# The last contraction chunk of a feature tile and of a key or query tile, side by side in the two halves of TensorE's rows

## The chip, the core and the metric

The kernel runs on one core of one Trainium2 chip. The metric is the device time of one execution in microseconds (us); the time before is the median of three runs. The engines named below are TensorE (PE; its weight loads are shown apart as PEld), VectorE (DVE), ScalarE (ACT), GpSimd (POOL) and SyncE (SP), which here only issues DMA transfers.

## What is computed

Two branches work on the same 2048 rows of `x`, with 448 features: linear attention with 16 heads of width 28, and a dense layer with a squared ReLU (1792 hidden features). A gate per row mixes them. Cut to what matters:

```python
g = sigmoid((x * gate_w).sum(-1, keepdims=True))
q, k, v = split(x @ wqkv)                    # 448 -> 3 * 448, 16 heads
phi = lambda t: where(t > 0, t + 1, exp(t)) + 1e-6
kv  = einsum("bhsd,bhse->bhde", phi(k), v);  z = phi(k).sum(over s)
a = (phi(q) @ kv / (phi(q) @ z + 1e-6)) @ wo
h = maximum(x @ w1 + b1, 0) ** 2             # 448 -> 1792
b = h @ w2 + b2                              # 1792 -> 448
out = g * a + (1 - g) * b
```

## The kernel before

**Precision by splitting.** Matrices are multiplied as `float32r`. To keep float32 precision each operand is kept as a high part and a low part (the rest), so a product of two 128-row chunks takes three matmuls: high by high, high by low, low by high.

**The contraction of 448.** Products with `x` (feature tiles of the dense layer, keys, queries) contract over 448 = 3 x 128 + 64. Chunks 0 to 2 have three matmuls each. The last chunk has 64 rows only, and the host puts them there twice, in partitions 0 to 63 and again in 64 to 127 (`twice`, L751). On chip the first copy of the weights is kept as high parts and the second as low parts (`split_w`, L126), while of `x` one tile holds high over low and the other low over high (`split_last`, L76). So two matmuls over all 128 rows (`xh[:, 3]` and `xl[:, 3]` against `w[:, 3]`) make all four products of the last chunk. A tile of outputs takes 3 x 3 + 2 = 11 matmuls.

**Three kinds of such tiles.** `up(b, f)` (L244) makes a feature tile: 128 hidden features by a block of 512 rows of `x`, moving operand 512 wide, into a PSUM bank `h_ps`; `hidden` (L234) then lets ACT take ReLU and square, and DVE split the result. `keys(t)` (L283) makes a tile of 128 rows by 448 keys, moving operand 448 wide, in `k_ps`. `queries(b, c)` (L433) makes 128 query columns by 512 rows in `q_ps`; its tile `c = 3` is narrower in precision (7 matmuls) and has a swap of partitions through DMAs. `keys` and `queries` return their later steps, which stand in the list `todo` until `run_todo` (L514) runs them: `phi` (L278, an exponential on ACT and two operations on DVE), for keys also splits (`rest`, L303), for queries the sum for the denominator.

**Other matmuls.** `down(b, f)` (L252) adds the products of feature tile `f` with `w2` to four accumulators `o_ps` (12 matmuls, 448 wide). `gram` (L320) sums the products of `x` and keys, `attention` (L497) applies the attention matrix to the scaled queries, `kv_product` (L385) and `m_product` (L411) build that matrix, `key_sums` makes `z_ps`, `denominators` makes `d_ps`. At L179 TensorE is kept busy with 15 matmuls until data arrives.

**Order.** The order on PE, ACT and DVE is written by hand (`manual_schedule`, L172): each engine runs its instructions in the order of the program's text. DMAs wait in SP's queue in program order too. The start (L521 to L595) treats block 0; the first half (L597) treats blocks 1 to 3, each with seven feature tiles `f`: `run_todo`, `up(b, f)`, `down` of the feature tile before, then a key tile for `f < 4` or `gram` after that. The second half (L656) takes the blocks in the order 3, 0, 1, 2 with the other seven feature tiles; there `up` and `down` alternate with `queries`, `scaled` (L485), `attention` and `finish` (L268). PSUM has eight banks: four `o_ps`, two for `up` (`mm`), and two (`ms0`, `ms1`) that keys, gram, queries and attention take in turn through `bank` (L48).

**What the steps below touch:** `split_w` and `split_wq` (last chunk), `terms_x`, `terms_w`, `products`, `up`, `keys`, `queries`, `run_todo`, `split_den` (L467), and the calls in the three stages. Working buffers in SBUF are slots of one pool (`slot`, L54): a load waits until the last reader of its slot is done.

Of the kernel before, what the change touches and what calls it, by code (L numbers as in the profile page):

```python
# [8 lines left out]
R = mybir.dt.float32r  # L9
# [6 lines left out]
P = 128  # L16
TB = 512
# [13 lines left out]
def gated_mix_kernel(ctx: ExitStack, tc: tile.TileContext, xt, xn, wk, wq, wv, wo, w1a, w1b, w2, b1, b2, gw, hmask,  # L31
# [28 lines left out]

    def split_hi(eng, hi, src):
        if eng is act:
            act.activation(hi, src, AF.Copy)  # L65
        elif eng is pool:
            pool.tensor_scalar(hi, src, 1.0, 0.0, op0=ALU.mult, op1=ALU.add)
        else:
            eng.tensor_copy(hi, src)  # L69
# [8 lines left out]
        dve.scalar_tensor_tensor(straight, src, sign[:, 1:2], f32(crossed), op0=ALU.mult, op1=ALU.subtract)  # L78
        split_lo(dve, crossed, src, straight)

    def products(out_ps, terms):
        n = len(terms)
        for i, (a, b) in enumerate(terms):
            pe.matmul(out_ps, a, b, start=(i == 0), stop=(i == n - 1))  # L84


    def terms_x(xh, xl, cols, w, wcols, c):
        if c == 3:
            return [(xh[:, 3, cols], w[:, 3, wcols]), (xl[:, 3, cols], w[:, 3, wcols])]
        return [(xh[:, c, cols], w[:, c, wcols]), (xh[:, c, cols], w[:, 4 + c, wcols]),  # L90
                (xl[:, c, cols], w[:, c, wcols])]

    def terms_w(xh, xl, w, wcols):
        t = []
        for c in range(3):
            t += [(w[:, c, wcols], xh[:, c]), (w[:, c, wcols], xl[:, c]), (w[:, 4 + c, wcols], xh[:, c])]
        return t + [(w[:, 3, wcols], xh[:, 3]), (w[:, 3, wcols], xl[:, 3])]

# [19 lines left out]
        else:  # L118
            split_last(xh[:, 3], xl[:, 3], r, side)

    def split_w(w, c, src, hi_eng, lo_eng):
        split_hi(hi_eng, w[:, c], src)
        if c < 3:
            split_lo(lo_eng, w[:, 4 + c], src, w[:, c])
        else:
            split_lo(lo_eng, w[64:, 3], src[64:], w[64:, 3])  # L126


    w1_s, w1_raw = {}, {}
# [6 lines left out]

    def new_w1(h, g):
        n, a, z = ((TB, 0, 16), (3 * P, 48, 0))[g]
        w = keep.tile([P, a + 7 * n + z], R, name=f"w1_{h}{g}", tag=f"w1{g}", bufs=1)
        w1_s[h, g] = w[:, a:a + 7 * n].rearrange("p (c n) -> p c n", c=7)  # L140
        return w1_s[h, g]

    def split_w1(h, g, c):
# [97 lines left out]
        split_lo(dve, lo, r, h)  # L241
        hs[f] = (h, lo)

    def up(b, f):  # L244
        ps = mm_p.tile([P, 512], F, name=f"h_ps{b}_{f}", tag="mm")
        for c in range(4):
            up_chunk(ps, b, f, c)
        hidden(ps, b, f)

    o_ps = {}  # L250
# [29 lines left out]
        dve.tensor_scalar(r, ps, 0.0, 1e-6, op0=ALU.max, op1=ALU.add)  # L280
        dve.scalar_tensor_tensor(p, e, 1.0, r, op0=ALU.min, op1=ALU.add)  # L281

    def keys(t):  # L283
        b, i = divmod(t, 4)
        if t < 2:
            ps = (acc_p, mm_p)[t].tile([P, 512], F, name=f"k_ps{t}", tag=("acc", "mm")[t])
        else:
            ps = bank(f"k_ps{t}")
        products(ps[:, :D], [term for c in range(4)
                             for term in terms_x(*xs[b], slice(i * P, (i + 1) * P), wk_s, slice(0, D), c)])  # L290
        e = slot([P, D], F, f"e{t}")
        r = slot([P, D], F, f"r{t}")
        p = r
        ph = tmp_p.tile([P, D], R, name=f"ph{t}", tag="ph", bufs=4)
        pl = tmp_p.tile([P, D], R, name=f"pl{t}", tag="pl", bufs=4)

        if t == 0:
            pool.memset(tmp_p.tile([P, 48], F, name="off"), 0.0)

        def first():  # L300
            phi(ps[:, :D], e, r, p)

        def rest():  # L303
            nh = tmp.tile([P, 512], R, name=f"nh{t}", tag="nh", bufs=4)
            nl = tmp.tile([P, 384], R, name=f"nl{t}", tag="nl", bufs=4)
            raw = xn_raw.pop(t)
            split_hi(act, nh[:, :D], raw)
            split_lo(pool, nl, raw[:, :384], nh[:, :384])
            split_lo(pool, nh[:, D:], raw[:, 384:], nh[:, 384:D])
            dve.scalar_tensor_tensor(e, raw, 1.0, gw_s, op0=ALU.mult, op1=ALU.mult, accum_out=logit[:, t:t + 1])  # L310
            split_hi(act, ph, p)
            split_lo(dve, pl, p, ph)
            if t == 0:
                pool.tensor_copy(ksum, p)
            else:
                pool.tensor_tensor(ksum, ksum, p, op=ALU.add)  # L316
            pend[t] = (ph, pl, nh, nl)
        return [first, rest]
# [15 lines left out]
                dve.tensor_tensor(gsum[c], ps[:, :D], gsum[c], op=ALU.add)  # L334
        return [after]

    wq_s = keep.tile([P, 8 + 7 * TB], R, name="wq_s")[:, 8:]
    wq_s = wq_s.rearrange("p (c n) -> p c n", c=7)
    wq_raw = {}

    def load_wq(c):
# [5 lines left out]
    def split_wq(c):  # L347
        raw = wq_raw.pop(c)
        split_hi(act, wq_s[:, c], raw)
        if c < 3:  # L350
            split_lo(dve, wq_s[:, 4 + c, :384], raw[:, :384], wq_s[:, c, :384])
        else:
            split_lo(dve, wq_s[64:, 3, :384], raw[64:, :384], wq_s[64:, 3, :384])
# [76 lines left out]

    pq, qs, den = {}, {}, {}

    def queries(b, c):  # L433
        ps = bank(f"q_ps{b}_{c}")
        xh, xl = xs[b]
        cols = slice(c * P, (c + 1) * P)
        if c < 3:
            products(ps, terms_w(xh, xl, wq_s, cols))
        else:
            products(ps, [(wq_s[:, i, cols], x[:, i]) for i in range(4) for x in ((xh, xl) if i < 3 else (xh,))])  # L440
        e = slot([P, TB], F, f"qe{b}_{c}")
        r = slot([P, TB], F, f"qr{b}_{c}")
        v = slot([P, TB], F, f"qv{b}") if c == 3 else None
        pq[b, c] = e

        def after():
            phi(ps if c < 3 else v, e, r, e)
            if (b, "s") not in den:
                den[b, "s"] = slot([P, TB], F, f"ds{b}")
                dve.tensor_scalar(den[b, "s"], e, zc[:, c:c + 1], None, op0=ALU.mult)  # L450
            else:
                dve.scalar_tensor_tensor(den[b, "s"], e, zc[:, c:c + 1], den[b, "s"], op0=ALU.mult, op1=ALU.add)  # L452
# [12 lines left out]
        return [swap if c == 3 else after]  # L465
# [45 lines left out]

    todo = []

    def run_todo():  # L514
        now, todo[:] = sorted(todo, key=lambda step: step.__name__ == "join"), []
        for step in now:
            todo.extend(step() or ())

# [22 lines left out]
                up_chunk(first[f], 0, f, c)  # L541
    split_w2(0)
    split_w2(1)
    wk_s = keep.tile([P, 7, D], R, name="wk_s", tag="wkm", bufs=1)
    for c in range(4):
        split_w(wk_s, c, wk_raw[c], act, dve)
    load(gw_s, gw.partition_broadcast(P))
    load(b2_s, b2.partition_broadcast(P))
    hidden(first[0], 0, 0)
# [18 lines left out]
    load_w2(4)  # L568
    load_x(1, 0)
    run_todo()  # L570
    up(0, 4)
    down(0, 2)
    todo += keys(2)
    load_xn(3)
    load_w2(5)
    load_x(1, 1)
    split_w2(4)
    run_todo()
    up(0, 5)
    down(0, 3)  # L580
    todo += keys(3)
    load_w2(6)
    load_x(1, 2)
    split_x(1, 0)
# [12 lines left out]
    for b in range(1, NB):  # L597
        for f in range(NH):
            run_todo()
            up(b, f)  # L600
            if f == 0:
                down(b - 1, NH - 1)
                half_done(b - 1)
                if b == 1:
                    for c in range(1, 4):
# [6 lines left out]
            if f < 4:  # L612
                if f < 3:
                    load_xn(4 * b + f + 1)
                todo += keys(4 * b + f)
            elif f < 6:
                todo += gram(b, f - 4)
            else:
# [37 lines left out]
    for n, b in enumerate(order):  # L656
        then = order[n + 1] if n + 1 < NB else None
        for f in range(NF - NH, NF):
            fl = f - NH
            run_todo()  # L660
            if fl == (0 if n else 4) and n != 1:
                split_den(b)
            up(b, f)
            if fl == 0 and n == 1:
                split_den(b)
            if then is not None and n and fl < 2:
                load_x(then, 2 * fl)
                load_x(then, 2 * fl + 1)
# [27 lines left out]
            else:  # L696
                down(order[n - 1], NF - 1)
                for i in range(4):
                    if n == 1:
                        attention(order[0], i)  # L700
                    finish(order[n - 1], i)
            if n == 0:
                if fl < 4:
                    todo += queries(b, (3, 0, 1, 2)[fl])
                if fl == 0:
                    for c in range(4):
                        load_w1(1, 1, c)
# [3 lines left out]
                    m_s = keep.tile([P, 7, D], R, name="m_s", tag="wkm", bufs=1)  # L711
                    split_kv(raw)
                    for j in range(2):
                        load_wo(j)
# [4 lines left out]
                if fl >= 4:  # L719
                    for c in ((3,), (0,), (1, 2))[fl - 4]:  # L720
                        todo += queries(then, c)
                if fl == 4:
                    todo += denominators(b)
                elif 2 <= fl < 6:
# [1 line left out]
            else:  # L726
# [7 lines left out]
                if then is not None and 3 <= fl:  # L734
                    todo += queries(then, (3, 0, 1, 2)[fl - 3])
    last = order[-1]
    down(last, NF - 2, range(3))
    for i in range(4):
# [55 lines left out]
```

## Time and profile before

| what | value |
|---|---|
| median of three runs | 437.86 us (437.72 to 438.6) |
| the profiled execution, its own time | 437.56 us |
| span of that execution, first to last instruction | 435.8 us |
| TensorE clock granted | 1.000 |
| DVE busy / ACT busy / POOL busy | 286.5 / 174.0 / 70.7 us |
| matmuls in the program | 2051 |
| DMA traffic | 29.00 MB in 18459 packets, mean 67 GB/s |

The page of the profile gives each engine's busy time as a share of the span. Matmuls are pipelined and the ends in the records are modelled: successive ones overlap, so a matmul's own duration is longer than the time between two starts, and it is the latter that adds up to the span. The chain of waits follows the work that ended last backwards, and gives for each piece its start, its length and its count; a piece of eleven matmuls divided by eleven is that time between starts.

### The profile page before, as it was taken

The page shows a single profiled execution, that of the slowest core. Times are in us where ns is not written, and L with a number is a line of the kernel's source. Part 1 is how long each engine was busy: PE and PEld are TensorE (multiplying, and loading weights), DVE is VectorE, ACT ScalarE, POOL GpSimd, SP SyncE. Part 2 cuts the span into 40 slices and gives each one's busy share as a digit, 9 for nine tenths or more (in the row PEclk, how much of TensorE's full clock was granted, in tenths as well). Part 3 has the DMA queues.
Part 4 walks back from the last instruction along what each step waited for, and adds up shares of the span by engine and source line. Part 5 has one row for each costly group of instructions (what it writes and reads, how often), then busy time and mean ns, then how long its engine had stood idle before and what let it go on. Part 6 is the DMA issues. An engine that isn't in the chain of part 4 may idle for free.

```text
span 435.8 us, 5547 instructions
## 1 busy us (share of the span) xinstructions
PE 430.4 (99%) x2051; PEld 380.7 (87%) x2051; DVE 286.5 (66%) x460; ACT 174.0 (40%) x301; POOL 70.7 (16%) x92
## 2 busy tenths in 40 slices
PE   9999999999999999999999999999999999999996
PEld 6888999898989898889888888888888888888985
DVE  5999537743779337883459778877653967457624
ACT  5855323421436123452245543444423434233421
POOL 0045013500234002540011342000100001000000
PEclk9999999999999999999999999999999999999999
DMA  7742202020131211132233321130101301002002
GB/s 271 249 133 70 89 0 70 25 68 28 42 120 31 68 45 64 49 84 84 80 123 112 71 62 37 55 128 0 26 0 48 135 0 26 0 0 86 0 2 84
DMA packets 18459, 29.00 MB, mean 67 GB/s; under 512 B 2896, under 2 KB 12928, under 8 KB 18432
## 3 DMA queue, kind: packets, MB, share of 16 engines
q1 hardware_dynamic: 16704, 26.51, 19.0%
q0 software_dynamic: 1728, 2.13, 2.3%
q8 instruction: 16, 0.26, 0.3%
q14 instruction: 11, 0.09, 0.1%
HBM read 22.31 MB, written 3.67 MB: 60 GB/s over the span
## 4 chain that ended last, share of the span: by engine, by line
PE 93%; DVE 4%; ACT 1%; DMA 1%; issue 0%; DVEq 0%; ACTq 0%
PE h_ps L232 31%; PE o_ps L261 30%; PE g_ps L84 8%; PE k_ps L84 8%; PE q_ps L84 7%; PE a_ps L84 7%; PE warm_ps L180 1%; PE kv_ps L389 1%; DVE qe L281 1%; DMA w2r<-in_w 1%; PE m_ps L84 1%; DVE ds L452 1%; DVE ql L72 0%; PE d_ps L84 0%; DVE qe L490 0%; DVE qr L280 0%
## 5 line engine op out<-in xcount | busy, mean ns | idle before, releaser
L261 PE MATMUL o_ps<-w,hh 128*128 128x448 f32 x448 | 126.1, 362 | 0.1
L232 PE MATMUL h_ps<-xh,w 128*128 128x512 f32 x392 | 126.2, 393 | 0.0
L261 PEld LDWEIGHTS o_ps<-w,hh 128*128 128x128 f32 x448 | 84.0, 187 | 9.2 <-DVE w L72 0.5
L232 PEld LDWEIGHTS h_ps<-xh,w 128*128 128x128 f32 x392 | 73.8, 189 | 15.2 <-DVE w L69 0.4
L232 PE MATMUL h_ps<-xl,w 128*128 128x512 f32 x224 | 86.9, 390 | 0.0
L261 PE MATMUL o_ps<-w,hl 128*128 128x448 f32 x224 | 81.3, 363 | 0.0
L236 ACT ACTIVATE hr<-h_ps,b_s 128x512 f32<-128x512 f32 x56 | 38.0, 679 | 77.6 <-PE h_ps L232 72.3
L69 DVE CAST hh<-hr 128x512 fp32r<-128x512 f32 x56 | 24.3, 434 | 48.0 <-ACT hr L237 47.9
L232 PEld LDWEIGHTS h_ps<-xl,w 128*128 128x128 f32 x224 | 42.2, 188 | 8.0
L261 PEld LDWEIGHTS o_ps<-w,hl 128*128 128x128 f32 x224 | 42.0, 188 | 2.7
L72 DVE TENSOR_TENSOR hl<-hr,hh 128x512 fp32r<-128x512 f32 x56 | 38.9, 694 | 3.1
L237 ACT ACTIVATE hr<-hr 128x512 f32<-128x512 f32 x56 | 35.4, 632 | 1.8
L72 POOL TENSOR_TENSOR nl<-xnr,nh 128x384 fp32r<-128x384 f32 x16 | 16.4, 1023 | 120.6 <-ACT nh L65 120.6
L84 PE MATMUL q_ps<-xh,wq_s 128*128 128x512 f32 x100 | 33.2, 390 | 0.0
L84 PE MATMUL a_ps<-m_s,qh 128*128 128x448 f32 x112 | 32.9, 363 | 0.2 <-ACT u L509 0.2
L84 PE MATMUL k_ps<-wk_s,xh 128*128 128x448 f32 x112 | 32.6, 361 | 0.0
L459 POOL DMA_DIRECT2D qr<-qv x16 | 8.1, 515 | 122.8 <-ACT qv L456 122.8
L280 DVE TENSOR_SCALAR r<-k_ps 128x448 f32<-128x448 f32 x16 | 10.0, 623 | 21.9 <-ACT e L279 21.9
L84 PE MATMUL q_ps<-xl,wq_s 128*128 128x512 f32 x60 | 23.5, 391 | 0.0
L72 DVE TENSOR_TENSOR pl<-r,ph 128x448 fp32r<-128x448 f32 x16 | 23.4, 1463 | 0.0
L316 POOL TENSOR_TENSOR ksum<-ksum,r 128x448 f32<-128x448 f32 x15 | 23.0, 1533 | 1.8 <-DVE r L281 1.8
L84 PE MATMUL a_ps<-m_s,ql 128*128 128x448 f32 x64 | 23.2, 363 | 0.0
(106 smaller groups left out, 578.3 us busy)
## 6 DMA issues: line engine op xcount, KB each, us to landing
xr<-in_xt SPq DMA_DIRECT2D x28, 256.0 KB, 2.7
xnr<-in_xn SPq DMA_DIRECT2D x16, 224.0 KB, 2.5
out<-out SPq DMA_DIRECT2D x16, 224.0 KB, 1.9
w2r<-in_w SPq DMA_DIRECT2D x14, 224.0 KB, 2.8
w1r<-in_w1a SPq DMA_DIRECT2D x7, 256.0 KB, 2.8
w1r<-in_w1b SPq DMA_DIRECT2D x8, 192.0 KB, 3.5
m_s<-m POOLq DMA_DIRECT2D x12, 112.0 KB, 2.4
wqr<-in_wq SPq DMA_DIRECT2D x4, 256.0 KB, 2.7
```

What stands on the lines that cost most here:

```text
L69: eng.tensor_copy(hi, src)
L72: eng.tensor_tensor(lo, src, f32(hi), op=ALU.subtract)
L84: pe.matmul(out_ps, a, b, start=(i == 0), stop=(i == n - 1))
L180: pe.matmul(warm_ps[:, :256], warm[:, :P], warm, start=True, stop=True)
L232: pe.matmul(ps, a, m, start=(c == 0 and n == 0), stop=(c == 3 and n == 1))
L236: act.activation(r, ps, AF.Relu, bias=b1_s[:, f:f + 1])
L237: act.activation(r, r, AF.Square)
L261: pe.matmul(o_ps[i][:, :D], a, m, start=(f % NH == 0 and n == 0), stop=(f % NH == NH - 1 and n == 2))
L280: dve.tensor_scalar(r, ps, 0.0, 1e-6, op0=ALU.max, op1=ALU.add)
L281: dve.scalar_tensor_tensor(p, e, 1.0, r, op0=ALU.min, op1=ALU.add)
L316: pool.tensor_tensor(ksum, ksum, p, op=ALU.add)
L459: pool.dma_start(out=r[p + 16:p + 32], in_=v[p:p + 16])
```

## The change

The last chunk of 25 feature tiles and of 25 key or query tiles is no longer done as 2 + 2 matmuls over all 128 rows. The feature tile now has three matmuls over rows 0 to 63 (high by high, high by low, low by high), the key or query tile three over rows 64 to 127, and they are issued in turn, one of the feature tile, one of the other. They write two different PSUM banks. Both tiles' chunks 0 to 2 come ahead of them. The fourth product, low by low, is dropped there. Of the 16 key tiles, numbers 2 to 15 are paired, and of the 12 query tiles with `c < 3` all but one; 14 + 11 = 25.

For this the weights of the last chunk need their low parts in both halves: a slot 7 is added to `w1`, `wk_s` and `wq_s`, with one more DVE operation over 64 rows for each of the six weight tiles. The order is changed so that a key or query tile stands beside its feature tile, ahead of `down` instead of behind it; `phi` of a query tile is run right after. The host code asks for a smaller scratch area of the GpSimd queue's DMA descriptors (8192 bytes a partition).

```diff
-    def products(out_ps, terms):
+    def products(out_ps, terms, whole=True):
         n = len(terms)
         for i, (a, b) in enumerate(terms):
-            pe.matmul(out_ps, a, b, start=(i == 0), stop=(i == n - 1))
+            pe.matmul(out_ps, a, b, start=(i == 0), stop=(whole and i == n - 1))
...
-    def split_w(w, c, src, hi_eng, lo_eng):
+    def split_w(w, c, src, hi_eng, lo_eng, his=slice(0, 64), los=slice(64, P)):
         split_hi(hi_eng, w[:, c], src)
         if c < 3:
             split_lo(lo_eng, w[:, 4 + c], src, w[:, c])
         else:
-            split_lo(lo_eng, w[64:, 3], src[64:], w[64:, 3])
+            split_lo(lo_eng, w[his, 7], src[his], w[his, 3])
+            split_lo(lo_eng, w[los, 3], src[los], w[los, 3])
...
-    def up(b, f):
+    def up(b, f, beside=None):
         ps = mm_p.tile([P, 512], F, name=f"h_ps{b}_{f}", tag="mm")
-        for c in range(4):
+        for c in range(3):
             up_chunk(ps, b, f, c)
+        if beside is None:
+            up_chunk(ps, b, f, 3)
+        else:
+            g, i = divmod(f % NH, 4)
+            w = w1_s[f // NH, g][:, 3, i * P:(i + 1) * P]
+            xh, xl = [x[:, 3] for x in xs[b]]
+            a = [(w[:64], xh[:64]), (w[:64], xl[:64]), (w1_s[f // NH, g][:64, 7, i * P:(i + 1) * P], xh[:64])]
+            other, most, terms = beside
+            products(other, most, False)
+            for n in range(3):
+                pe.matmul(ps, *a[n], start=False, stop=(n == 2))
+                pe.matmul(other, *terms[n], start=False, stop=(n == 2))
         hidden(ps, b, f)
...
-    def keys(t):
+    def keys(t, f=None):
...
+            up(b, f, (ps[:, :D], terms, [(xl[64:, 3, cols], wk_s[64:, 3]), (xh[64:, 3, cols], wk_s[64:, 3]),
+                                         (xl[64:, 3, cols], wk_s[64:, 7])]))
...
-    def queries(b, c):
+    def queries(b, c, f=None):
...
+                up(f[0], f[1], (ps, terms, [(w[64:], xl[64:, 3]), (w[64:], xh[64:, 3]), (wq_s[64:, 7, cols], xl[64:, 3])]))
...
-    def run_todo():
-        now, todo[:] = sorted(todo, key=lambda step: step.__name__ == "join"), []
-        for step in now:
-            todo.extend(step() or ())
+    def run_todo(joins=True):
+        steps = sorted(todo, key=lambda step: step.__name__ == "join")
+        todo[:] = [step for step in steps if step.__name__ == "join" and not joins]
+        for step in steps:
+            if step not in todo:
+                todo.extend(step() or ())
...
-    wk_s = keep.tile([P, 7, D], R, name="wk_s", tag="wkm", bufs=1)
+    wk_s = keep.tile([P, 8, D], R, name="wk_s", tag="wkm", bufs=1)
     for c in range(4):
-        split_w(wk_s, c, wk_raw[c], act, dve)
+        split_w(wk_s, c, wk_raw[c], act, dve, slice(64, P), slice(0, 64))
...
-    up(0, 4)
+    todo += keys(2, 4)
     down(0, 2)
-    todo += keys(2)
...
-            up(b, f)
+            if f < 4:
+                k_first, k_rest = keys(4 * b + f, f)
+                todo.append(k_first)
+            else:
+                up(b, f)
             if f == 0:
                 down(b - 1, NH - 1)
+                if b == 1:
+                    run_todo()
                 half_done(b - 1)
...
-            run_todo()
+            run_todo(n or fl not in (1, 5))
             if fl == (0 if n else 4) and n != 1:
                 split_den(b)
-            up(b, f)
-            if fl == 0 and n == 1:
-                split_den(b)
+            beside = {}
+            if n == 0:
+                beside = {1: (b, 0), 2: (b, 1), 3: (b, 2), 5: (then, 0), 6: (then, 1)}
+            elif then is not None:
+                beside = {4: (then, 0), 5: (then, 1), 6: (then, 2)}
+            if fl in beside:
+                todo += queries(*beside[fl], (b, f))
+                run_todo(False)
+            else:
+                up(b, f)
...
                     if n == 1:
                         attention(order[0], i)
+                        if i == 1:
+                            split_den(b)
...
-                if fl < 4:
-                    todo += queries(b, (3, 0, 1, 2)[fl])
                 if fl == 0:
+                    todo += queries(b, 3)
+                    run_todo()
                     for c in range(4):
                         load_w1(1, 1, c)
...
-    nc = bacc.Bacc("TRN2", target_bir_lowering=False, num_devices=1)
+    nc = bacc.Bacc("TRN2", target_bir_lowering=False, num_devices=1, dynamic_dma_scratch_size=8192)
```

Not shown: `keys` and `queries` without `f` do their last chunk as before (two matmuls over 128 rows), `split_wq` gets the same extra operation as `split_w`, and the later calls of `queries` in the second half are moved to match.

More of the change, by code (lines that the diff above doesn't have):

```diff
@@ L79, in split_last @@
         split_lo(dve, crossed, src, straight)
-    def products(out_ps, terms):
+    def products(out_ps, terms, whole=True):
         n = len(terms)
         for i, (a, b) in enumerate(terms):
-            pe.matmul(out_ps, a, b, start=(i == 0), stop=(i == n - 1))
+            pe.matmul(out_ps, a, b, start=(i == 0), stop=(whole and i == n - 1))
     def terms_x(xh, xl, cols, w, wcols, c):
-        if c == 3:
-            return [(xh[:, 3, cols], w[:, 3, wcols]), (xl[:, 3, cols], w[:, 3, wcols])]
         return [(xh[:, c, cols], w[:, c, wcols]), (xh[:, c, cols], w[:, 4 + c, wcols]),
@@ L96, in terms_w @@
             t += [(w[:, c, wcols], xh[:, c]), (w[:, c, wcols], xl[:, c]), (w[:, 4 + c, wcols], xh[:, c])]
-        return t + [(w[:, 3, wcols], xh[:, 3]), (w[:, 3, wcols], xl[:, 3])]
+        return t
     x_raw, xs = {}, {}
@@ L138, in new_w1 @@
         n, a, z = ((TB, 0, 16), (3 * P, 48, 0))[g]
-        w = keep.tile([P, a + 7 * n + z], R, name=f"w1_{h}{g}", tag=f"w1{g}", bufs=1)
-        w1_s[h, g] = w[:, a:a + 7 * n].rearrange("p (c n) -> p c n", c=7)
+        w = keep.tile([P, a + 8 * n + z], R, name=f"w1_{h}{g}", tag=f"w1{g}", bufs=1)
+        w1_s[h, g] = w[:, a:a + 8 * n].rearrange("p (c n) -> p c n", c=8)
         return w1_s[h, g]
@@ L288, in keys @@
             ps = bank(f"k_ps{t}")
-        products(ps[:, :D], [term for c in range(4)
-                             for term in terms_x(*xs[b], slice(i * P, (i + 1) * P), wk_s, slice(0, D), c)])
+        (xh, xl), cols = xs[b], slice(i * P, (i + 1) * P)
+        terms = [term for c in range(3) for term in terms_x(xh, xl, cols, wk_s, slice(0, D), c)]
+        if f is None:
+            products(ps[:, :D], terms + [(x[:, 3, cols], wk_s[:, 3]) for x in (xl, xh)])
+        else:
+            up(b, f, (ps[:, :D], terms, [(xl[64:, 3, cols], wk_s[64:, 3]), (xh[64:, 3, cols], wk_s[64:, 3]),
+                                         (xl[64:, 3, cols], wk_s[64:, 7])]))
         e = slot([P, D], F, f"e{t}")
@@ L335, in gram @@
         return [after]
-    wq_s = keep.tile([P, 8 + 7 * TB], R, name="wq_s")[:, 8:]
-    wq_s = wq_s.rearrange("p (c n) -> p c n", c=7)
+    wq_s = keep.tile([P, 8 + 8 * TB], R, name="wq_s")[:, 8:]
+    wq_s = wq_s.rearrange("p (c n) -> p c n", c=8)
     wq_raw = {}
@@ L352, in split_wq @@
         else:
-            split_lo(dve, wq_s[64:, 3, :384], raw[64:, :384], wq_s[64:, 3, :384])
+            split_lo(dve, wq_s[64:, 7, :384], raw[64:, :384], wq_s[64:, 3, :384])
+            split_lo(dve, wq_s[:64, 3, :384], raw[:64, :384], wq_s[:64, 3, :384])
         second = [t[:, 384:].rearrange("p (j r) -> p j r", j=NJ)[:, :, 16:] for t in (wq_s[:, c], raw)]
@@ L437, in queries @@
         if c < 3:
-            products(ps, terms_w(xh, xl, wq_s, cols))
+            terms, w = terms_w(xh, xl, wq_s, cols), wq_s[:, 3, cols]
+            if f is None:
+                products(ps, terms + [(w, xl[:, 3]), (w, xh[:, 3])])
+            else:
+                up(f[0], f[1], (ps, terms, [(w[64:], xl[64:, 3]), (w[64:], xh[64:, 3]), (wq_s[64:, 7, cols], xl[64:, 3])]))
         else:
@@ L578, in gated_mix_kernel @@
     run_todo()
-    up(0, 5)
+    todo += keys(3, 5)
     down(0, 3)
-    todo += keys(3)
     load_w2(6)
@@ L599, in gated_mix_kernel @@
             run_todo()
-            up(b, f)
+            if f < 4:
+                k_first, k_rest = keys(4 * b + f, f)
+                todo.append(k_first)
+            else:
+                up(b, f)
             if f == 0:
                 down(b - 1, NH - 1)
+                if b == 1:
+                    run_todo()
                 half_done(b - 1)
@@ L614, in gated_mix_kernel @@
                     load_xn(4 * b + f + 1)
-                todo += keys(4 * b + f)
+                todo.append(k_rest)
             elif f < 6:
@@ L659, in gated_mix_kernel @@
             fl = f - NH
-            run_todo()
+            run_todo(n or fl not in (1, 5))
             if fl == (0 if n else 4) and n != 1:
                 split_den(b)
-            up(b, f)
-            if fl == 0 and n == 1:
-                split_den(b)
+            beside = {}
[6 more added lines that the diff above has]
+                run_todo(False)
+            else:
+                up(b, f)
             if then is not None and n and fl < 2:
@@ L710, in gated_mix_kernel @@
                     late = ctx.enter_context(tc.tile_pool(name="late", bufs=1, side="right", reuse_waits="tile"))
-                    m_s = keep.tile([P, 7, D], R, name="m_s", tag="wkm", bufs=1)
+                    m_s = keep.tile([P, 8, D], R, name="m_s", tag="wkm", bufs=1)[:, :7]
                     split_kv(raw)
@@ L718, in gated_mix_kernel @@
                     scaled(b, c)
-                if fl >= 4:
-                    for c in ((3,), (0,), (1, 2))[fl - 4]:
-                        todo += queries(then, c)
+                if fl in (4, 6):
+                    todo += queries(then, {4: 3, 6: 2}[fl])
+                if fl == 4:
+                    run_todo()
                 if fl == 4:
@@ L733, in gated_mix_kernel @@
                     attention(b, i)
-                if then is not None and 3 <= fl:
-                    todo += queries(then, (3, 0, 1, 2)[fl - 3])
+                if then is not None and fl == 3:
+                    todo += queries(then, 3)
     last = order[-1]
```

## The prediction

> **What bounds the kernel now.** I read the page first, its busy times and its chain of work that ended last.
>
> ```profile
> span 435.8 us, 5547 instructions
> PE 430.4 (99%) x2051; PEld 380.7 (87%) x2051; DVE 286.5 (66%) x460; ACT 174.0 (40%) x301; POOL 70.7 (16%) x92
> PE 93%; DVE 4%; ACT 1%; DMA 1%; issue 0%; DVEq 0%; ACTq 0%
> ```
>
> PE is busy 99% of the span and is 93% of the chain. That alone doesn't prove a bound, since the ends of matmuls are modelled, so I went on to the chain in order of time (start, length, what, count). Two stretches, from the first half and from the second:
>
> ```profile
> 31.91 2.49 PE h_ps L232 x11
> 34.40 2.41 PE o_ps L261 x12
> 36.81 2.20 PE k_ps L84 x11
> ...
> 308.98 2.49 PE q_ps L84 x11
> 311.48 2.49 PE h_ps L232 x11
> ```
>
> Each piece begins where the last ends. The steps between starts are 2.49/11 = 227 ns for a 512-wide matmul, and 2.20/11 = 200 ns for a 448-wide one. TensorE walks through the program at these steps, and whatever shortens its list shortens the kernel, if nothing else becomes late. The groups of the page show how much longer one matmul is than its step:
>
> ```profile
> L232 PE MATMUL h_ps<-xh,w 128*128 128x512 f32 x392 | 126.2, 393 | 0.0
> L389 PE MATMUL kv_ps<-gsum,wv 128*112 128x112 f32 x32 | 3.3, 262 | 0.0
> ```
>
> One 512-wide matmul lasts 393 ns and is followed after 227: 166 ns of it lie under the next one.
>
> **The change, part by part.** A feature tile and its partner take 2 + 2 matmuls for their last chunks now: with a key tile 2 x 227 + 2 x 200 = 854 ns, with a query tile 4 x 227 = 908 ns. Afterwards there are three pairs. If the two of a pair run side by side, a pair takes the step of its longer one, 227 ns, and the three take 681. The gross gain is 173 ns for each of 14 key tiles (2.42 us) and 227 ns for each of 11 query tiles (2.50 us), 4.92 us in all.
>
> No 64-row matmul stands in this trace, so three costs need bounds: how far the pair overlaps, the skew with which the second of a pair starts, and the two switches between 128-row and 64-row work. The nearest rows are the place where PE goes from one shape to another, the attention matrix's product into a feature tile (timeline of PE; merged entries show start, time covered, count):
>
> ```profile
> 220.96 0.66 PE L389 MATMUL kv_ps<-gsum,wv 128*112 128x112 f32 x5
> 221.38 0.48 PE L232 MATMUL h_ps<-xh,w 128*128 128x512 f32 x1
> 221.70 0.39 PE L232 MATMUL h_ps<-xl,w 128*128 128x512 f32 x1
> ...
> 201.96 0.95 PE L368 MATMUL z_ps<-ones,zk 128*128 128x2 f32 x8
> 202.76 0.48 PE L232 MATMUL h_ps<-xh,w 128*128 128x512 f32 x1
> ```
>
> The five products last 262 ns each and cover 0.66 us, so the fifth starts at 220.96 + 0.66 - 0.26 = 221.36, a step of 100 ns. The feature tile's first matmul starts 20 ns later, at 221.38, and its second at 221.70: 340 ns after the fifth product, where the two ordinary steps are 100 + 227 = 327. This switch of shape cost 13 ns. **Switch:** its bounds are 0 and 166 ns (PE runs empty before the other shape may start, so that the covered part of a matmul is laid open); I take 20, rounded up from the nearest row. **Skew:** the closest two starts here are these 20 ns apart. The other end is 100: the eight `z_ps` matmuls stream only two columns each and yet start (202.76 - 201.96)/8 = 100 ns apart, which is what a weight load of its own takes. Two loads, 200 ns, just fit under the last 128-row matmul of 200 or 227 ns, so I take 20. The same 200 ns for two loads stays under the 227 of a pair. **Overlap:** bounds are 227 ns a pair and both matmuls one after the other, 427 or 454; I take 227, since the loads fit and the two write different banks.
>
> A group then takes 681 + 20 + 2 x 20 = 741 ns. That saves 113 ns with a key tile (14 x 113 = 1.58 us) and 167 ns with a query tile (11 x 167 = 1.84 us): **3.42 us**.
>
> Only a page has a price for the overlap itself. The Trainium skill, "TensorE: Matmul & The Clock Gate", section "Measured speedup vs the span model", reports 3.07 times the speed for four 32-row tiles at 512 columns; read as 77% of the ideal, it would make an estimated 227/0.77 = 295 ns a pair and 3 x 68 x 25 = 5.1 us less gain. No row here shows it.
>
> **The start.** DVE gets one operation more for each of three weight tiles there.
>
> ```profile
> L72 DVE TENSOR_TENSOR w<-w1r,w 64x512 fp32r<-64x512 f32 x2 | 1.4, 691 | 0.1
> L72 DVE TENSOR_TENSOR wk_s<-wkr,wk_s 64x448 fp32r<-64x448 f32 x1 | 0.6, 624 | 0.0
> L72 DVE TENSOR_TENSOR w<-w1r,w 64x384 fp32r<-64x384 f32 x2 | 1.1, 556 | 0.1
> ...
> 4.00:38.00 34.00, 33.91 (x157) 29.30 (x155) 31.50 (x51) 23.11 (x43) 8.89 (x9) 1.00 0.64 208
> ...
> 13.38 2.35 DVE L72 TENSOR_TENSOR wk_s<-wkr,wk_s 128x448 fp32r<-128x448 f32 x4
> 15.76 0.43 DVE L69 CAST hh<-hr 128x512 fp32r<-128x512 f32 x1
> 16.22 0.69 DVE L72 TENSOR_TENSOR hl<-hr,hh 128x512 fp32r<-128x512 f32 x1
> ...
> 17.24 0.56 PE L261 MATMUL o_ps<-w,hh 128*128 128x448 f32 x2
> 17.64 0.36 PE L261 MATMUL o_ps<-w,hl 128*128 128x448 f32 x1
> ...
> 26.78 0.93 PE L261 MATMUL o_ps<-w,hh 128*128 128x448 f32 x2
> 27.55 0.36 PE L261 MATMUL o_ps<-w,hl 128*128 128x448 f32 x1
> ```
>
> The window's third pair is DVE: 31.50 of 34 us busy, so there is little cover. Two operations, 0.69 + 0.62 = 1.31 us, come ahead of the first split of a hidden tile. Its high part moves from 16.19 to 17.50 and its low part from 16.91 to 18.22, while PE asks for them at 17.24 and 17.64: PE loses 0.26 and then, from 17.90, another 0.32, so **+0.6** (bounds 0 and 1.31). At 26.78 PE already waits for DVE: its two matmuls take 0.77 us to the third start instead of 0.40. There DVE comes 0.69 + 0.62 + 0.56 = 1.87 us later, but the 128-row matmuls of key tile 2 (9 x 200 ns) and one pair more than before now stand ahead of this `down`: PE comes some 2.0 us later too, plus the 0.6. The old stall goes, **-0.37** (bounds -0.37 and, with the order's cover gone, +1.5). The other three extra operations, 0.56 to 0.69 us each, lie where DVE has room (its share of the span is 66%).
>
> **The second half's order.** At its second block PE waits, by the rows:
>
> ```profile
> 275.51 0.65 PE L84 MATMUL a_ps<-m_s,qh 128*128 128x448 f32 x2
> 276.00 0.36 PE L84 MATMUL a_ps<-m_s,ql 128*128 128x448 f32 x1
> ...
> 279.80 0.36 PE L84 MATMUL a_ps<-m_s,ql 128*128 128x448 f32 x1
> 280.38 0.67 PE L84 MATMUL a_ps<-m_s,qh 128*128 128x448 f32 x2 [0.21 <-ACT u L509]
> 280.89 0.36 PE L84 MATMUL a_ps<-m_s,ql 128*128 128x448 f32 x1
> ...
> 279.17 0.63 ACT L65 ACTIVATE dh<-ds 128x512 fp32r<-128x512 f32 x1 [3.64 <-DVE ds L452]
> 279.71 1.14 ACT L509 ACTIVATE u<-a_ps,gate 128x448 f32<-128x448 f32 x2
> ```
>
> The steps 0.49, 0.58 and 0.51 stand for 0.40, 0.20 and 0.40: 0.58 us lost, say **-0.57** to be had. ACT is held by `dh`, which waits for the sums of two query tiles, and only then reads the attention bank. Afterwards one of these query tiles is done before, and `split_den` comes behind the second attention tile. What is late next is the first attention tile: `phi` of query tile 1 now precedes three `scaled` on DVE, which has the same total to do. I count the stall as gone; left as it is, or doubled, it moves the sum by 0.6 up or 1.1.
>
> **At no cost.** The changed order adds waits in PE's own queue: a feature tile's last matmuls stand behind its partner's, which need the bank's earlier reader to be done. That reader is `phi` of two tiles before, run one feature tile (7.1 us by the chain's three pieces) ahead. If it were late, `hidden` and the next `down` would be. The swap's DMAs move ahead of other loads in SP's queue:
>
> ```profile
> 208.21 8.81 SPq L58 DMA_DIRECT2D w1r<-in_w1b  x4
> 223.39 2.50 SPq L58 DMA_DIRECT2D qr<-qv  x4
> ...
> 216.86 1.61 PE q_ps L84 x7
> ...
> 245.16 2.51 PE h_ps L232 x11
> ```
>
> They wait for the query tile's end at 218.5 and ACT's copy, so the four `w1r` loads behind them slip to some 222; their first use, the fifth feature tile at 245, leaves 20 us. The smaller descriptor area touches GpSimd's few transfers only.
>
> **Sum:** -3.42 + 0.6 - 0.37 - 0.57 = -3.76 us. The profiled execution took 437.56 us, which gives 433.8; the median is 0.3 above it, and carried to the median the forecast is **434.1**.
>
> **Rivals.**
>
> *Each switch empties TensorE* (the slower side). Before the first 64-row matmul and after the last, the 166 ns that now lie covered are laid open: 681 + 20 + 332 = 1033 ns a group, +179 with a key tile, +125 with a query tile, +3.88 us, with the other terms **441.4**. It decides from (4.92 us/25 - 20)/2 = 88 ns a switch. For it: two sizes of work share one array, and half the rows start fresh. Against: the switch in the rows above cost 13 ns; but both of its shapes use all rows. The Trainium skill, "TensorEngine Tiling (Array Packing)", section "Key Properties", has this rule: changing the tiling mode drains the engine. No run here shows a 64-row mode, so the rule keeps a real chance. A load of 100 ns laid open in each pair gives about the same.
>
> *The second half's weights load only when the first has started.* Skew 100: 821 ns, -33 and -87, -1.42 us, in all **436.1**. For it: nearly every load in the rows goes one matmul ahead, no more.
>
> *No side by side* (the change doesn't do what it says). Six steps instead of four: +427 and +454 ns, +10.97 us, in all **448.5**. Against: nothing but the different rows and banks.
>
> *The gain is given back*, at the start by DVE or by switches of some 70 ns: about **437.9**.
>
> **Chances.** Forecast 0.50, late weights 0.13, emptying 0.22, no overlap 0.08, given back 0.07. The range leaves out the no-overlap case and little else: from 432.2 (gross gain without any cost of the pairs) to 441.5. Where cheap switches hold, the time lies within 432.2 to 436.4. About 0.2% (0.9 us) is what a measurement of this kernel tells from no change. Faster by more: 0.60; within: 0.11; slower by more: 0.29.
>
> **What would show it.** In the changed profile a pair's two starts some 20 ns apart, pairs 227 ns apart, and no gap ahead of the first pair or behind the last confirm the main term. Gaps of 150 ns or more on both sides of each group are the emptying; starts 113 ns apart with six evenly spaced would still be side by side, 200 ns apart would not. A `down` at 17 us that waits for DVE, no wait at the third `down`, and none in the first attention tiles confirm the small terms. A new wait of PE for a query or key bank would make the order's part wrong.

## The result, and the profile after

The changed kernel takes **444.04 us** (443.6 to 444.22, four runs) against 437.79 (437.54 to 438.6): a ratio of 1.0138 with an interval of 1.012 to 1.0156. It is slower by 6.2 us, on the other side of the forecast and above its range. First the page of the changed kernel, its span and busy times and the share of its chain by engine.

```profile
span 442.3 us, 5653 instructions
PE 436.4 (99%) x2101; PEld 372.1 (84%) x2101; DVE 281.9 (64%) x466; ACT 173.0 (39%) x301; POOL 71.3 (16%) x92
PE 96%; DVE 1%; DMA 1%; ACT 1%; issue 0%; POOL 0%; DVEq 0%; ACTq 0%
```

TensorE is the bound as before, even more so; it simply walks for longer, though four matmuls of a group have become three pairs. So I looked at one group, a key tile beside a feature tile, in the order of time. First the matmuls of PE (start, length, what), then the weight loads.

```profile
66.62 0.37 PE L86 MATMUL k_ps<-wk_s,xl 128*128 128x448 f32 x1
66.91 0.49 PE L259 MATMUL h_ps<-xh,w 64*128 64x512 f32 x1
66.92 0.47 PE L260 MATMUL k_ps<-wk_s,xl 64*128 64x448 f32 x1
67.23 0.36 PE L260 MATMUL k_ps<-wk_s,xh 64*128 64x448 f32 x1
67.25 0.39 PE L259 MATMUL h_ps<-xl,w 64*128 64x512 f32 x1
67.43 0.36 PE L260 MATMUL k_ps<-wk_s,xl 64*128 64x448 f32 x1
67.48 0.39 PE L259 MATMUL h_ps<-xh,w 64*128 64x512 f32 x1
67.80 0.67 PE L274 MATMUL o_ps<-w,hh 128*128 128x448 f32 x2
68.31 0.37 PE L274 MATMUL o_ps<-w,hl 128*128 128x448 f32 x1
```

```profile
66.42 0.19 PEld L86 LDWEIGHTS k_ps<-wk_s,xl 128*128 128x128 f32 x1
66.91 0.18 PEld L259 LDWEIGHTS h_ps<-xh,w 64*128 64x128 f32 x1 [0.31 <-issue]
66.92 0.18 PEld L260 LDWEIGHTS k_ps<-wk_s,xl 64*128 64x128 f32 x1
...
67.80 0.30 PEld L274 LDWEIGHTS o_ps<-w,hh 128*128 128x128 f32 x2 [0.36 <-issue]
```

The pairs do run side by side: their starts are 10 to 50 ns apart. But look at the two edges.

- **Going in.** The last 128-row matmul starts at 66.62; its 448 columns take a step of 0.20, so the next is due at 66.82 and starts at 66.91. Its weights, elsewhere loaded one matmul ahead (the load at 66.42 is for the matmul at 66.62), are loaded at 66.91 as well, when it starts. So it lasts 0.49 instead of 0.39, and the second pair comes 0.34 later instead of 0.23.
- **Inside.** From the second pair to the third the feature tile needs 67.48 - 67.25 = 0.23: the ordinary step of 227 ns.
- **Coming out.** The next 128-row matmul starts 0.32 after the third pair instead of 0.23, again together with its own load, and the two `o_ps` starts up to 68.31 take 0.51 instead of 0.40.

From the last key matmul at 66.62 to the third of `down` at 68.31 there are 1.69 us. Without the three ordinary steps of 0.20 the group has taken 1.09 us, where the four matmuls took 0.854. The query groups show the same edges, with 1.10 us instead of 0.908. For all groups the profile gives 14 x (1.093 - 0.854) + 11 x (1.097 - 0.908) = **5.4 us**. The waits for weights confirm it over all groups (who waited, for whom, us in total, times, longest):

```profile
PEld h_ps L259 <- issue: 8.2, 25, 0.4
PEld o_ps L274 <- issue: 8.0, 22, 0.4
PEld q_ps L86 <- ACT qv L479: 1.2, 1, 1.2
```

In 25 groups the load at the way in comes late, in 22 the one at the way out (for three others the view names a result of DVE, at most 0.4 us each), and no semaphore explains them ("issue").

The third row is a second loss, once, in the second half's first block. PE's timeline:

```profile
258.55 0.39 PE L233 MATMUL h_ps<-xh,w 128*128 128x512 f32 x1
259.70 0.50 PE L86 MATMUL q_ps<-xh,wq_s 128*128 128x512 f32 x1 [0.76 <-ACT qv L479]
```

and ACT's around it:

```profile
254.08 0.57 ACT L67 ACTIVATE woh<-wor 112x448 fp32r<-112x448 f32 x1
258.62 0.54 ACT L67 ACTIVATE m<-m_ps 128x448 fp32r<-128x448 f32 x1 [3.98 <-DMA m_s<-m]
259.06 0.58 ACT L479 COPY qv<-q_ps 128x512 f32<-128x512 f32 x1
```

PE starts 1.15 us after the matmul before instead of 0.23. It waits for the bank that ACT empties with the copy `qv`; the copy stands behind the split of the attention matrix's third product, and ahead of that split ACT stands idle for 3.98 us, up to the end of the transfers that read the only buffer `m`. With the step after it, which is 0.11 us too long, PE loses 1.03 us.

### The profile page after: what moved, and what is told of

It is laid out like the page before. It is cut to its first block, busy times and chain, and to the rows that moved or that the text cites. A ratio compares the mean times of both kernels' runs of the same rounds, so it can differ in the third digit from the quotient of the medians.

```text
span 442.3 us, 5653 instructions
## 1 busy us (share of the span) xinstructions
PE 436.4 (99%) x2101; PEld 372.1 (84%) x2101; DVE 281.9 (64%) x466; ACT 173.0 (39%) x301; POOL 71.3 (16%) x92
## 4 chain that ended last, share of the span: by engine, by line
PE 96%; DVE 1%; DMA 1%; ACT 1%; issue 0%; POOL 0%; DVEq 0%; ACTq 0%
PE o_ps L274 31%; PE h_ps L233 28%; PE a_ps L86 8%; PE g_ps L86 8%; PE q_ps L86 7%; PE k_ps L86 7%; PE h_ps L259 4%; PE k_ps L260 1%; PE warm_ps L181 1%; PE kv_ps L408 1%; DMA m_s<-m 1%; PE d_ps L86 0%; POOL m_s L445 0%; PE m_ps L86 0%; PE z_ps L387 0%
## 5 line engine op out<-in xcount | busy, mean ns | idle before, releaser
L274 PE MATMUL o_ps<-w,hh 128*128 128x448 f32 x448 | 128.7, 368 | 0.0
L233 PE MATMUL h_ps<-xh,w 128*128 128x512 f32 x367 | 120.7, 393 | 0.0
L233 PEld LDWEIGHTS h_ps<-xh,w 128*128 128x128 f32 x367 | 69.0, 189 | 14.9 <-DVE w L74 0.4
L233 PE MATMUL h_ps<-xl,w 128*128 128x512 f32 x199 | 77.3, 391 | 0.0
L233 PEld LDWEIGHTS h_ps<-xl,w 128*128 128x128 f32 x199 | 37.4, 188 | 6.8
L74 POOL TENSOR_TENSOR nl<-xnr,nh 128x384 fp32r<-128x384 f32 x16 | 18.7, 1166 | 99.3 <-ACT nh L67 72.4
L86 PE MATMUL q_ps<-xh,wq_s 128*128 128x512 f32 x89 | 30.9, 391 | 0.8 <-ACT qv L479 0.8
L86 PE MATMUL k_ps<-wk_s,xh 128*128 128x448 f32 x98 | 27.7, 362 | 0.0
L86 PE MATMUL g_ps<-pl,nh 128*128 128x448 f32 x64 | 23.2, 362 | 0.0
L532 ACT ACTIVATE u<-a_ps,gate 128x448 f32<-128x448 f32 x16 | 10.2, 635 | 33.1 <-PE a_ps L86 33.1
```

The source lines that it names most:

```text
L74: eng.tensor_tensor(lo, src, f32(hi), op=ALU.subtract)
L86: pe.matmul(out_ps, a, b, start=(i == 0), stop=(whole and i == n - 1))
L233: pe.matmul(ps, a, m, start=(c == 0 and n == 0), stop=(c == 3 and n == 1))
L274: pe.matmul(o_ps[i][:, :D], a, m, start=(f % NH == 0 and n == 0), stop=(f % NH == NH - 1 and n == 2))
L532: act.activation(u, ps[:, :D], AF.Copy, scale=gate[:, 0, t:t + 1])
```

## The experiments

Two theories stood against each other at first. **S**: the switches between 128-row and 64-row work cost the 5.4 us. **O**: the new order and the extra operations on weights cost most of it. Rival P put the cost into the pairs themselves.

**The order without the pairs.** All of the change stays except the pairs:

```diff
-            other, most, terms = beside
-            products(other, most, False)
-            for n in range(3):
-                pe.matmul(ps, *a[n], start=False, stop=(n == 2))
-                pe.matmul(other, *terms[n], start=False, stop=(n == 2))
+            up_chunk(ps, b, f, 3)
+            products(*beside)
...
```

> The changed order, buffers and extra weight operations stay; the last chunks of the 25 pairs of tiles are done as before, two 128-row matmuls each. Theory S (switches): the whole group of three pairs takes 1.09 to 1.10 us in the changed kernel where the four matmuls took 0.855 and 0.908, so 14 x 0.237 + 11 x 0.189 = 5.4 us of the 6.2 lost come from the switches between 128-row and 64-row work; this run gives 438.6 us. Rival O (order): the new order and the extra operations cost most of it; 441 us or more.

Measured: 437.34 us, ratio 0.9989 (0.998 to 0.9999). The order and the extra operations cost nothing together; O falls. It came out 1.3 us below what S had expected; by its timeline PE's wait for the query bank (1.03 us) and the delays in the attention tiles (0.3 us) are not there either.

**A lone 64-row matmul** in each of 52 feature tiles of the kernel before:

```diff
-            terms = [(w[:, 3, cols], xh[:, 3]), (w[:, 3, cols], xl[:, 3])]
+            terms = [(w[:, 3, cols], xh[:, 3]), (w[:rows, 3, cols], xl[:rows, 3])]
...
-            up_chunk(ps, b, f, c)
+            up_chunk(ps, b, f, c, rows=64)
```

> The kernel before, with the last matmul of 52 feature tiles over rows 0 to 63 only (the low-weight by high-x product of the last chunk is left out there). The number of matmuls stays. Theory S: each of the 52 lone 64-row matmuls pays two switches, together 0.41 us as in the changed kernel's groups, so about +21 us, 459 us. Rival P (64-row matmuls are slow only because two run side by side): no change, 437.8 us.

Measured: 457.66 us, ratio 1.0452 (1.0436 to 1.0467), +19.7 us. One of them in PE's timeline:

```profile
72.77 0.61 PE L232 MATMUL h_ps<-xh,w 128*128 128x512 f32 x2
73.31 0.50 PE L232 MATMUL h_ps<-xl,w 64*128 64x512 f32 x1
73.74 0.68 PE L261 MATMUL o_ps<-w,hh 128*128 128x448 f32 x2
74.25 0.36 PE L261 MATMUL o_ps<-w,hl 128*128 128x448 f32 x1
```

Two steps of 0.23 from 72.77 would bring it to 73.22: it starts 0.09 late, lasts 0.50, and the matmul after it comes 0.43 later instead of 0.23, the two after that take 0.51 instead of 0.40. That is 0.09 + 0.20 + 0.11 = 0.40 us for one 64-row matmul with nothing beside it, 52 x 0.40 = 20.8 us. The kernel as a whole lost 1.1 us less; by its timeline the waits of the kernel before at the third `down` and in the attention tiles, 0.9 us, are gone in this run. The cost is there with nothing to pair; P falls.

**Twice the pairs, the same switches:**

```diff
-            for n in range(3):
-                pe.matmul(ps, *a[n], start=False, stop=(n == 2))
-                pe.matmul(other, *terms[n], start=False, stop=(n == 2))
+            for n in range(6):
+                pe.matmul(ps, *a[n % 3], start=False, stop=(n == 5))
+                pe.matmul(other, *terms[n % 3], start=False, stop=(n == 5))
```

> The changed kernel with each group's three pairs issued twice in a row (the last chunk is counted twice). Theory S: a pair that does not follow a switch takes 235 ns, as the third pair of each group does in the trace, so 25 x 3 x 0.235 = +17.6 us, 461.6 us. Rival P: every pair takes a third of 1.095 us, 365 ns, so +27.4 us, 471.4 us.

Measured: 461.51 us, ratio 1.0541 (1.0525 to 1.0556). That is 17.5 us over the changed kernel's 444.04, or 17.5/75 = 233 ns for each additional pair. A pair that follows no switch costs its longer step and almost nothing more.

**Ninety-six rows.** The lone matmul again, with one number changed:

```diff
-            up_chunk(ps, b, f, c, rows=64)
+            up_chunk(ps, b, f, c, rows=96)
```

> As the lone 64-row matmul of 52 feature tiles, but over rows 0 to 95 (of the last matmul's second half, rows 96 to 127 are left out). Theory S: what is paid for is the change between work on all rows and work on one half; 96 rows don't fit in a half and are done as whole-array work, as the 112-row matmuls of the attention matrix are, which keep the step of 200 ns; so no loss, 437.9 us. Rival R (any other number of rows empties TensorE): 457.7 us as with 64 rows.

Measured: 438.84 us, ratio 1.0023 (1.0014 to 1.0032). By the timeline a load goes one matmul ahead here, as for 128 rows:

```profile
64.25 0.19 PEld L232 LDWEIGHTS h_ps<-xl,w 96*128 96x128 f32 x1
64.47 0.42 PEld L261 LDWEIGHTS o_ps<-w,hh 128*128 128x128 f32 x2
...
64.47 0.40 PE L232 MATMUL h_ps<-xl,w 96*128 96x512 f32 x1
64.70 0.57 PE L261 MATMUL o_ps<-w,hh 128*128 128x448 f32 x2
```

The remaining 0.9 us is 18 ns for each of 52 matmuls, against 0.38 us (19.7/52) with 64 rows. So not every other number of rows costs: 96 rows run next to 128 at almost no price, 64 rows don't. The 18 ns stand for the way in and the way out together, for which I had forecast 40. Row numbers other than 64 and 96 were not tried in this place.

**The halves one after the other.** The loop of the pairs becomes two loops:

```diff
             for n in range(3):
                 pe.matmul(ps, *a[n], start=False, stop=(n == 2))
+            for n in range(3):
                 pe.matmul(other, *terms[n], start=False, stop=(n == 2))
```

> The changed kernel with the same 64-row matmuls, but the three of the feature tile first and the three of its partner behind them instead of in turn. Theory S, the two halves run side by side and going from one half to the other is no switch: the partner's first can still start beside the third of the feature tile, and its other two add 2 x 200 (keys) or 2 x 227 ns (queries), +10.6 us, 454.6 us. Rival N (nothing runs side by side unless weights were loaded in turn): three whole steps are added, 14 x 0.600 + 11 x 0.681 = +15.9 us, 459.9 us.

Measured: 443.94 us, ratio 1.0139 (1.0125 to 1.0152): the same as in turn, which neither theory had expected. The timeline of PE for the group shown above:

```profile
66.82 0.49 PE L259 MATMUL h_ps<-xh,w 64*128 64x512 f32 x1
66.83 0.47 PE L261 MATMUL k_ps<-wk_s,xl 64*128 64x448 f32 x1
67.15 0.36 PE L261 MATMUL k_ps<-wk_s,xh 64*128 64x448 f32 x1
67.16 0.39 PE L259 MATMUL h_ps<-xl,w 64*128 64x512 f32 x1
67.35 0.36 PE L261 MATMUL k_ps<-wk_s,xl 64*128 64x448 f32 x1
67.39 0.39 PE L259 MATMUL h_ps<-xh,w 64*128 64x512 f32 x1
```

The key matmuls (L261) stand behind all three of the feature tile in the program, and yet the first starts 10 ns after the feature tile's first. The two halves work off their matmuls each for itself. My theory of this run fell; the one on the switches doesn't need it.

**One part alone.** The pairs of keys only, and of queries only; the other kind has its last chunk as two 128-row matmuls at the same place. The edit of the first run, in `queries`; the second makes the same one in `keys`:

```diff
-                up(f[0], f[1], (ps, terms, [(w[64:], xl[64:, 3]), (w[64:], xh[64:, 3]), (wq_s[64:, 7, cols], xl[64:, 3])]))
+                up(*f)
+                products(ps, terms + [(w, xl[:, 3]), (w, xh[:, 3])])
```

> The changed kernel with the 14 key pairs alone; the query tiles stand at the same places but do their last chunk as two 128-row matmuls. Theory S: the kernel in the changed order without pairs took 437.3 us; 14 groups add 14 x 0.237 = 3.3 us: 440.7 us. If groups cost by what surrounds them and not each by itself, the two parts (keys alone, queries alone) won't add up to the whole.

> The changed kernel with the 11 query pairs alone; the key tiles do their last chunk as two 128-row matmuls. Theory S: 437.3 + 11 x 0.189 = 439.4 us, and with the wait of PE for the query bank (1.0 us) and in the attention tiles (0.3 us), if pairs of queries bring these about, 440.7 us.

Measured: 440.39 us with keys alone (ratio 1.0055, 1.0038 to 1.0072) and 440.66 with queries alone (1.0063, 1.0048 to 1.0078). Over the 437.34 of the order without pairs that is 3.05 and 3.32, together 6.4; the whole has 6.7. The parts add up to within 0.3 us, and keys cost about what their 14 groups cost (3.3). Queries cost 1.2 us more than their 11 groups (2.1). By its timeline that kernel has the wait for the query bank (0.88 us with the step after it) and the delays in the attention tiles (0.30); the one with keys alone has neither.

**That wait.** First I suspected the swap of the query tile `c = 3`, which the change runs at once, ahead of other loads:

```diff
                     todo += queries(b, 3)
-                    run_todo()
...
-                if fl == 4:
-                    run_todo()
```

> The changed kernel, but in the second half's first block the swap of the query tile c = 3 waits for the next feature tile again, as before (the two immediate calls of run_todo are gone). If the moved swap made PE wait 0.9 us for ACT's copy, by way of later loads of x, a later split of the attention matrix and a late bank: 443.1 us. If not: 444.0 us.

Measured: 444.62 us, ratio 1.015 (1.0135 to 1.0166). No gain, and PE still waits for the copy, by the trace for longer. That story fell. The second concerned the queue of ACT: move the copy ahead of the split that waits for `m`.

```diff
-                if fl == 4:
-                    m_product(2)
...
                     run_todo()
+                    m_product(2)
```

> The changed kernel with one step moved: in the feature tile 4 of the second half's first block the query tile c = 3 and its copy by ACT come ahead of the attention matrix's third product instead of behind it. Theory M: the 1.03 us that PE loses at 258.5 us comes from ACT's queue, where the copy of the query bank stands behind a split that waits 4.0 us for the transfers out of the only buffer m; so 443.0 us. Rival: the bank is late for another reason, the moved order of the swap alone: 444.0 us as the changed kernel.

Measured: 443.64 us (442.75 to 444.37), ratio 1.013 (1.0117 to 1.0144). Against the changed kernel this is within the scatter, but in the trace PE's wait is gone and the split alone waits:

```profile
255.69 0.59 ACT L479 COPY qv<-q_ps 128x512 f32<-128x512 f32 x1 [1.15 <-PE q_ps L86]
258.35 0.55 ACT L67 ACTIVATE m<-m_ps 128x448 fp32r<-128x448 f32 x1 [2.08 <-DMA m_s<-m]
```

To settle it I took away what the split waits for, and ran the changed kernel again beside it:

```diff
-        m = late.tile([P, 2, D], R, name=f"m{j}", tag="m", bufs=1)
+        m = late.tile([P, 2, D], R, name=f"m{j}", tag="m", bufs=2)
```

> The changed kernel itself, again, beside the next one on the same chip: 444.0 us.

> The changed kernel with two buffers for m instead of one (the descriptor area is 7680 bytes instead of 8192, for room). Theory M: ACT's split of the attention matrix's third product no longer waits for the transfers out of the only m, the copy of the query bank behind it comes earlier, and PE's wait of 1.03 us at 258.5 us goes: 443.0 us. If it stays: 444.0 us.

Measured: 444.25 us for the changed kernel (444.05 to 446.02) and 443.35 with two buffers (443.13 to 444.94), 0.9 us between the medians. One high value in each set of four makes the ranges overlap, so the times alone don't settle it; and the descriptor area is smaller too (7680 bytes). But by the view of waits PE's only wait for a semaphore is now the one at the very start:

```profile
PE warm_ps L181 <- DVE part L178: 1.1, 1, 1.1
```

Both ways of taking the copy out from behind this wait remove PE's. So the chain is: one buffer `m`, its transfers, the split in ACT's queue, the copy behind it, the bank, PE.

**A version that beats both.** The kernel before in the changed order, without pairs, without slot 7 and its operations (edit against the changed kernel):

```diff
-            split_lo(lo_eng, w[his, 7], src[his], w[his, 3])
-            split_lo(lo_eng, w[los, 3], src[los], w[los, 3])
+            split_lo(lo_eng, w[64:, 3], src[64:], w[64:, 3])
...
+            up_chunk(ps, b, f, 3)
+            products(*beside)
...
```

> The kernel before in the changed order alone: two 128-row matmuls for every last chunk, no slot 7, no extra operations on weights, the descriptor area as before. The order takes away the waits of PE at the third down (0.37 us) and in the first attention tiles (0.57 us). Theory S expects 437.0 to 437.4 us, under both kernels by a little; if the order brings nothing by itself, 437.9 us.

Measured: median 437.14 us, ratio 0.9978 (0.9969 to 0.9987): faster than the kernel before by 0.2%. The waits in the attention tiles are gone from its timeline. The third `down`, where PE waited at 26.78 before, now follows its key tile without a break (chain of waits):

```profile
27.39 2.21 PE k_ps L86 x11
29.59 2.40 PE o_ps L266 x12
```

## Why the prediction was wrong

**What bounds the kernel: right.** The time followed PE's walk to the end; the span grew by 6.5 us and nearly all of it stands between PE's starts.

**Overlap and skew: right.** A pair was put at 227 ns; it takes 233 (twice the pairs). The skew was put at 20 ns; the first pair's starts are 10 apart. Of the gross gain of 4.92 us all but 25 x 3 x 6 ns = 0.45 us is there. The estimate of 295 ns a pair, worked out in the prediction from the Trainium skill, "TensorE: Matmul & The Clock Gate", section "Measured speedup vs the span model", did not come true.

**The switch: the step that failed.** I took 20 ns from the place where PE goes from the 112-column products to a feature tile, and called it the nearest row. Measured are 0.20 us at each edge and 0.41 a group, ten times that. At each edge the first matmul of the other kind starts about 0.09 us late, and the step after it is 0.11 too long. The prediction also let the first pair's two loads run under the last 128-row matmul; they start only with the pair itself, at 66.91 and 66.92. It said itself what was weak in the row, that both its shapes use all rows; the runs with 64 and 96 rows show that this matters.

The 0.11 could have been read before the change. After its wait at 280.38, a line of the prediction, PE takes 0.51 us to the third start instead of 0.40, and there too the load begins with its matmul (weight loads of the kernel before):

```profile
280.37 0.30 PEld L84 LDWEIGHTS a_ps<-m_s,qh 128*128 128x128 f32 x2 [0.58 <-ACT u L509]
```

By these rows the 0.11 is what a load costs that isn't ahead, at a switch as after a wait. The 0.09 has no such row in the kernel before; I read it as TensorE running empty.

The rival *each switch empties TensorE*, with a chance of 0.22, was right in kind. It put the emptying at 166 ns a switch, more than the 90 seen, and set no load beside it: in place of its 1033 ns a group took 1093 or 1097, 14 x 0.060 + 11 x 0.064 = 1.5 us more. The sign that it gave, gaps of 150 ns or more on both sides of a group, appears only when the late start and the long step are added. The rule that it named, from the Trainium skill, "TensorEngine Tiling (Array Packing)", section "Key Properties", that changing the tiling mode drains the engine, fits these traces: 0.09 us late at the way in and at the way out of each group.

**At no cost: wrong in one point.** For the banks I looked at `phi` as the earlier reader. The query tile `c = 3` has another reader, the copy `qv`, and ahead of that in ACT's queue stood a wait for a DMA. Why it got late can be read from ACT's timeline at the first query pair, in the changed kernel and then in the run of the order without pairs:

```profile
230.23 0.69 ACT L237 ACTIVATE hr<-h_ps,b_s 128x512 f32<-128x512 f32 x1 [3.79 <-PE h_ps L259]
...
231.97 1.75 ACT L67 ACTIVATE w<-w1r 128x384 fp32r<-128x384 f32 x4
```

```profile
224.37 0.69 ACT L237 ACTIVATE hr<-h_ps,b_s 128x512 f32<-128x512 f32 x1 [1.31 <-PE h_ps L233]
...
226.86 0.60 ACT L285 ACTIVATE qe<-q_ps 128x512 f32<-128x512 f32 x1 [1.14 <-PE q_ps L86]
227.35 1.75 ACT L67 ACTIVATE w<-w1r 128x384 fp32r<-128x384 f32 x4
```

Without pairs ReLU and square run under the query tile's matmuls, and the exponential starts as soon as those end; the splits begin 0.5 us after it starts. In a pair the feature tile ends together with its partner, and the splits begin 1.74 us after ReLU does, some 1.2 us later as seen from PE. From there the chain of the attention matrix through its one buffer runs late, and PE lost 1.03 us. That this delay is the first cause is read from the two timelines; no run tried it alone.

**The start: the size right, in this execution by luck.** The first `down` starts at 17.66 instead of 17.24, and PE waits 0.1 once more, +0.5 where +0.6 was forecast. But PE doesn't wait for DVE at the first `down`, as the prediction had it: the first key tile already starts 0.42 late. PE's timeline before, then after:

```profile
15.03 0.57 PE L84 MATMUL k_ps<-wk_s,xh 128*128 128x448 f32 x2
```

```profile
15.45 0.57 PE L86 MATMUL k_ps<-wk_s,xh 128*128 128x448 f32 x2
...
17.66 0.56 PE L274 MATMUL o_ps<-w,hh 128*128 128x448 f32 x2
...
19.46 0.66 PE L274 MATMUL o_ps<-w,hh 128*128 128x448 f32 x2
```

That tile's start differs between the runs' profiles, from 14.71 to 15.72; the version without the extra operations has 15.48. The wait for DVE is real all the same: in the second profile of the changed kernel PE loses 0.5 us in steps between 17.0 and 20.4. The wait at the third `down` is gone as forecast.

**The attention tiles: half right.** Of 0.57 us some 0.30 are left: by the rows, a step of 0.39 instead of 0.20 and then 0.50 for two instead of 0.40. They come with the pairs of queries; what delays these tiles was not followed further.

```profile
283.01 0.37 PE L86 MATMUL a_ps<-m_s,ql 128*128 128x448 f32 x1
283.40 0.67 PE L86 MATMUL a_ps<-m_s,qh 128*128 128x448 f32 x2
283.90 0.37 PE L86 MATMUL a_ps<-m_s,ql 128*128 128x448 f32 x1
```

Put together with the rival's 441.4: +1.5 for the groups, +1.0 for the query bank, +0.3 for the attention tiles give 444.2, and 444.04 was measured. The range ended at 441.5 because its upper end was this rival, with a group 60 ns too cheap and no wait for a bank.

Two smaller sums of the prediction don't come out by its own terms: the lower end of the range is 432.6 rather than 432.2, and switches of 70 ns would leave 436.6 rather than 437.9. Nothing above hangs on them.

## What to carry to other kernels

In these runs matmuls on one half of TensorE's rows came at a fixed price for each stretch of them, 0.40 to 0.41 us in and out for one matmul, three pairs and six pairs alike, so count stretches and not matmuls. Three pairs a stretch save 0.17 or 0.23 us and lose; with six the sum is 1.79 us against 1.71 for two key groups and 1.82 for two query groups (worked out from the runs, not tried), which is still no gain to speak of. And before an operation is called the reader that frees a bank, read what stands ahead of it in its own engine's queue.

## What the runs showed that I had not expected

- The two halves of TensorE's rows work through their matmuls independently: issued in series or in turn, the groups take the same time (443.94 and 444.04 us), and a matmul later in the program starts ahead of an earlier one of the other half. In the run with six pairs a half with 448 columns also keeps its own step of 0.20 us beside one with 512:

```profile
69.30 0.39 PE L259 MATMUL h_ps<-xl,w 64*128 64x512 f32 x1
69.49 0.36 PE L260 MATMUL k_ps<-wk_s,xl 64*128 64x448 f32 x1
69.54 0.39 PE L259 MATMUL h_ps<-xh,w 64*128 64x512 f32 x1
69.69 0.36 PE L260 MATMUL k_ps<-wk_s,xl 64*128 64x448 f32 x1
```

- At a switch the weights of the other mode aren't loaded ahead, in either direction. What TensorE does in the 0.09 us stays open, since starts and ends of matmuls are as the profile records and models them; shorter moving operands and quarters of the rows were not tried.
